# Three-piece score visits in batches 3 to 7, with a piece placed in two of TensorE's single PSUM banks

## The chip, the cores and the metric

One core of one Trainium2 chip. The metric is the time of one execution in device microseconds, the median of several runs. A ratio is the mean time of one kernel's fast runs over the mean of the fast runs of the kernel before from the same rounds, so it is not quite the ratio of the medians quoted beside it. A profile's span is some 1.7 us shorter than the time of its run. The profiled run of the kernel before took 342.69 us, 1.6 above its median. Microseconds are written us.

## The reference, cut to what matters

```python
B, H, S, Nb, D = 8, 8, 576, 16, 64
k_all = concat([beacon_k, k]); v_all = concat([beacon_v, v])     # 592 keys
scores = q @ k_all.T / sqrt(D), causal on the 576 ordinary keys  # ... per batch and head
a = exp(scores - max); a /= a.sum(-1)
x = (a @ v_all) as 4608 tokens x 512
h = relu(x @ w_in); out = (h * h) @ w_out                        # d_ff = 2048
```

Attention of eight batches feeds an MLP on all tokens. The MLP needs far more TensorE time than the attention, and the kernel lays the attention of one batch between MLP chunks of earlier ones.

## The kernel before

Every piece of work is an `Op`, and a list scheduler inside the Python program (`Order.run`) decides while the kernel is built in which order the operations of each engine stand. It plays with estimated durations, and it hands out PSUM banks from pools. PSUM is TensorE's output memory. The kernel divides it into eight banks: two "strips" of two banks for scores, and four single banks `ps` for everything else (MLP, values, transposes).

```python
strips = [psum.tile([128, 2, 512], FP32, name=f"strip{i}") for i in range(2)]
ps = [psum.tile([128, 512], FP32, name=f"ps{i}") for i in range(4)]
...
order = Order(pools={"strip": range(2), "ps": range(4), "stg": range(NSTG)}, limits={"av": 2, "tp": 2})
```

The scores of a batch (four pairs of heads) are cut into 13 pieces of 512 columns. For each piece TensorE makes 64-row matmuls for two heads side by side (one head in each bank of a strip), and ScalarE takes exp of both banks in one instruction of 1024 columns. A *visit* is a run of score matmuls on TensorE between other work; here it has up to two pieces, so a batch has seven visits.

```python
def emit_scores(b, mms, st):
    for pr, c, t0, t1, at in mms:
        for hj in range(2):
            nc.tensor.matmul(st[:, hj, at:at + t1 - t0], kT[b % 2][64*hj:64*hj+64, pr, ...],
                             qT[b % 2][64*hj:64*hj+64, pr, t0:t1], start=True, stop=True)

def add_exp(name, qk, s, at, width, prio):
    def emit(e):
        nc.scalar.activation(pt[:, :, at:at + width], strips[qk.slots[s]][:, :, 0:width], AF.Exp, ...)
    ...
            if len(parts) == 2 or n == NPC - 1 and b not in CROSS:
                opened.clear()                 # the visit is full
```

A single bank is filled by TensorE and then emptied ("evicted") by ScalarE or VectorE: ReLU of an MLP group, the reciprocal and the product that normalize the values, or a copy.

The softmax here doesn't subtract the row's maximum and nothing guards it: scores larger than these inputs give would overflow.

## Time and profile before

| | before |
|---|---|
| time, median | 341.06 us (340.79 to 341.26) |
| TensorE (PE) busy | 335.6 of 341.0 us, 98% |
| ScalarE (ACT), VectorE (DVE) busy | 56%, 51% |
| chain that ended last | 97% PE |
| score runs on PE in the built order | 65 |

The page of the kernel before: the busy line of section 1 (engine, busy us, share of the span, instructions) and the chain that ended last (section 4).

```profile
PE 335.6 (98%) x3197; PEld 187.4 (55%) x3197; DVE 173.0 (51%) x389; ACT 190.3 (56%) x270; POOL 92.5 (27%) x145
...
PE 97%; DVE 1%; issue 0%; ACT 0%; DVEq 0%
```

The view of waits of the same kernel, TensorE alone (who waited for whom: us in total, times, longest us). These three lines are all.

```profile
PE ps L286 <- DVE warm L293: 1.1, 1, 1.1
PE ps L878 <- DVE g L896: 0.7, 1, 0.7
PE ps L475 <- ACT g L894: 0.5, 1, 0.5
```

TensorE is the bound, and nearly all of its time is its own. A change helps if TensorE streams less or loses less between instructions, and a new wait of TensorE should be paid in full.

The chain of the kernel before in order of time shows what a visit looks like (start us, length us, what); L611 are scores, L715 values, L878 and L916 the MLP:

```profile
138.20 1.83 PE ps L916 x8
140.04 0.46 PE ps L715 x15
140.50 0.86 PE ps L916 x4
141.36 0.55 PE strip L611 x10
141.91 0.57 PE ps L715 x15
```

Four MLP matmuls of 512 columns take 0.86 us, fifteen value matmuls 0.46, but 0.57 after the visit at 141.36. Start times of single matmuls in the trace show the visit's fixed cost better: the last matmul before a visit lasts 0.096 us longer than its columns need, the visit's last pair 0.10 longer, and the first matmul after it 0.01 longer. That is 0.205 us for a visit of any size.

### The profile page before, as it was taken

The page shows a single profiled execution, that of the slowest core. Times are in us where ns is not written, and L with a number is a line of the kernel's source. Part 1 is how long each engine was busy: PE and PEld are TensorE (multiplying, and loading weights), DVE is VectorE, ACT ScalarE, POOL GpSimd, SP SyncE. Part 2 cuts the span into 40 slices and gives each one's busy share as a digit, 9 for nine tenths or more (in the row PEclk, how much of TensorE's full clock was granted, in tenths as well). Part 3 has the DMA queues.
Part 4 walks back from the last instruction along what each step waited for, and adds up shares of the span by engine and source line. Part 5 has one row for each costly group of instructions (what it writes and reads, how often), then busy time and mean ns, then how long its engine had stood idle before and what let it go on. Part 6 is the DMA issues. An engine that isn't in the chain of part 4 may idle for free.

```text
span 341.0 us, 7787 instructions
## 1 busy us (share of the span) xinstructions
PE 335.6 (98%) x3197; PEld 187.4 (55%) x3197; DVE 173.0 (51%) x389; ACT 190.3 (56%) x270; POOL 92.5 (27%) x145
## 2 busy tenths in 40 slices
PE   8999999999999999999999999999999999999996
PEld 7677665544564555555467855545454544444444
DVE  3886886238465982477336743767255502401400
ACT  2886765367647765576456653675367316514721
POOL 9773712406504533042315041504000000000000
PEclk9999999999999999999999999999999999999999
DMA  8999987999999999799989998997310131011003
GB/s 143 209 185 213 209 149 165 224 241 217 170 204 238 219 172 189 162 238 188 201 154 220 226 215 131 217 233 125 105 62 2 29 104 62 0 60 65 0 2 123
DMA packets 143953, 51.72 MB, mean 152 GB/s; under 512 B 130702, under 2 KB 138798, under 8 KB 143918
## 3 DMA queue, kind: packets, MB, share of 16 engines
q1 hardware_dynamic: 135375, 42.19, 61.8%
q0 software_dynamic: 7904, 8.69, 15.0%
q8 instruction: 25, 0.41, 0.5%
q10 hardware_dynamic: 639, 0.36, 0.4%
q14 instruction: 10, 0.08, 0.1%
HBM read 37.22 MB, written 9.44 MB: 137 GB/s over the span
## 4 chain that ended last, share of the span: by engine, by line
PE 97%; DVE 1%; issue 0%; ACT 0%; DVEq 0%
PE ps L878 36%; PE ps L916 36%; PE ps L715 9%; PE strip L611 9%; PE ps L286 3%; PE ps L475 2%; PE ps L782 1%; PE ps L828 1%; DVE g L903 1%; PE ps L472 0%; ACT g L894 0%; PE ps L420 0%; DVE g L896 0%; ACT osb L316 0%; DVE g L292 0%
## 5 line engine op out<-in xcount | busy, mean ns | idle before, releaser
L878 PE MATMUL ps<-xT,w_in 128*128 128x512 bf16 (+3 forms) x704 | 134.0, 340 | 0.7 <-DVE g L896 0.7
L916 PE MATMUL ps<-w_out,g 128*128 128x512 bf16 x560 | 131.4, 379 | 0.0
L620 ACT ACTIVATE pt<-strip 128x1024 bf16<-128x1024 f32 (+3 forms) x107 | 101.9, 1000 | 43.2 <-PE strip L611 42.8
L878 PEld LDWEIGHTS <-w_in 128*128 128x128 bf16 x704 | 65.5, 98 | 52.9 <-issue 2.0
L894 ACT ACTIVATE g<-ps 128x512 bf16<-128x512 f32 (+2 forms) x120 | 67.5, 563 | 45.2 <-PE ps L878 44.7
L903 DVE TENSOR_TENSOR g<-g 128x1024 bf16<-128x1024 bf16 (+2 forms) x80 | 54.2, 684 | 68.6 <-ACT g L894 67.7
L916 PEld LDWEIGHTS <-g 128*128 128x128 bf16 x560 | 51.0, 98 | 54.8 <-issue 1.7
L318 POOL CAST qk_area<-stg 128x512 bf16<-128x512 f32 (+2 forms) x60 | 40.1, 676 | 66.1 <-DMA stg<-in_q_dram 33.7
L318 POOL CAST vb<-stg 128x512 bf16<-128x512 f32 (+1 forms) x40 | 26.4, 671 | 67.8 <-DMA stg<-in_v_dram 49.3
L316 ACT COPY osb<-ps 128x512 f32<-128x512 f32 (+2 forms) x28 | 15.8, 567 | 50.8 <-PE ps L916 48.6
L715 PEld LDWEIGHTS <-pt 128*128 128x128 bf16 (+1 forms) x960 | 35.7, 98 | 11.0 <-issue 2.1
L715 PE MATMUL ps<-vb,pt 128*128 128x65 bf16 (+1 forms) x960 | 39.8, 194 | 0.0
L689 DVE TENSOR_TENSOR pt<-pt,tri 128x512 bf16<-128x512 bf16 x64 | 31.6, 503 | 10.2 <-ACT pt L620 9.0
L611 PE MATMUL strip<-qT,kT 64*128 64x208 bf16 (+15 forms) x596 | 34.2, 239 | 0.0
L734 DVE TENSOR_TENSOR xn<-ps,rcp 128x320 bf16<-128x320 f32 (+2 forms) x64 | 31.5, 492 | 2.3
L611 PEld LDWEIGHTS <-kT 64*128 64x128 bf16 x596 | 19.0, 94 | 21.2 <-issue 19.9
L732 DVE RECIPROCAL rcp<-ps 128x5 f32<-128x5 f32 (+2 forms) x64 | 12.2, 190 | 34.5 <-PE ps L715 34.2
L896 DVE TENSOR_SCALAR g<-ps 128x512 bf16<-128x512 f32 (+2 forms) x40 | 23.4, 601 | 8.6 <-PE ps L878 7.4
L318 DVE COPY osb<-ps 128x512 f32<-128x512 f32 (+1 forms) x10 | 6.5, 651 | 31.0 <-PE ps L916 19.0
L286 PE MATMUL ps<-g 128*128 128x256 bf16 (+1 forms) x83 | 12.0, 302 | 1.1 <-DVE warm L293 1.1
L362 POOL DMA_DIRECT2D stg<-in_v_dram x10 | 8.6, 866 | 6.4 <-DMA w_in<-in_moe_w_in_dram 5.3
L286 PEld LDWEIGHTS <-g 128*128 128x128 bf16 x83 | 7.9, 122 | 3.5 <-issue 1.5
(40 smaller groups left out, 82.2 us busy)
## 6 DMA issues: line engine op xcount, KB each, us to landing
out_dram<-osb SPq DMA_DIRECT2D x17, 512.0 KB, 4.3
stg<-in_q_dram SPq DMA_DIRECT2D x24, 256.0 KB, 5.0
stg<-in_k_dram SPq DMA_DIRECT2D x18, 256.0 KB, 5.3
stg<-in_v_dram SPq DMA_DIRECT2D x18, 256.0 KB, 4.7
w_in<-in_moe_w_in_dram POOLq DMA_DIRECT2D x4, 512.0 KB, 8.7
w_out<-in_moe_w_out_dram POOLq DMA_DIRECT2D x4, 512.0 KB, 11.2
stg<-in_v_dram POOLq DMA_DIRECT2D x6, 256.0 KB, 8.3
stg<-in_k_dram SPq DMA_DIRECT2D x6, 224.0 KB, 4.1
```

Of the source, the lines that this page charges most:

```text
L286: nc.tensor.matmul(ps[bank][:, 0:cols], g[1][:, 0, 0:128], g[1][:, 0, 0:cols], start=True, stop=True)
L318: eng[e].tensor_copy(dst, src)
L611: nc.tensor.matmul(st[:, hj, at:at + t1 - t0], kT[b % 2][hp, pr, 128 * c:128 * c + 128], qT[b % 2][hp, pr, t0:t1], start=True, stop=True,)
L620: nc.scalar.activation(pt[:, :, at:at + width], strips[qk.slots[s]][:, :, 0:width], AF.Exp, bias=0.0, scale=scale)
L689: nc.vector.tensor_tensor(out=d, in0=d, in1=tri[:, m0:m0 + m, :][:, None].to_broadcast([128, 2, m, 128]), op=ALU.min)
L715: nc.tensor.matmul(a[:, at + (t - tl[0]) * (D + 1):at + (t - tl[0] + 1) * (D + 1)], P[0:rr, hj, o:o + 128], vb[b % 2][0:rr, c, 2 * pr + hj ...
L734: nc.vector.tensor_tensor(out=xn[b % 2].rearrange("p t (h d) -> p h t d", d=D)[:, h0:h0 + nh, tl[0]:tl[0] + nt], in0=a[:, :, :, 0:D], in1= ...
L878: nc.tensor.matmul(h[:, lo - spans[0][0]:hi - spans[0][0]], w_in_sb[:, mc, ft * 128:(ft + 1) * 128], xT[:, mc, lo % RING:lo % RING + hi - lo],
L894: nc.scalar.activation(dst, h, AF.Relu, bias=0.0, scale=1.0)
L896: nc.vector.tensor_scalar(out=dst, in0=h, scalar1=0.0, scalar2=None, op0=ALU.max)
L903: nc.vector.tensor_tensor(out=d, in0=d, in1=d, op=ALU.mult)
L916: nc.tensor.matmul(o, G[:, fc, ts * 128:(ts + 1) * 128], w_out_sb[:, fc, :], start=(fc == 0), stop=(fc == NFT - 1))
```

## The change

Intent: fewer visits. In batches 3 to 7 the 13 pieces go in visits of 2, 3, 3, 3 and 2 pieces. The two strips hold two pieces, and the third goes into single banks 0 and 1 while a visit needs them. An exp reads two banks in one instruction, so the two banks are made halves of one tile. The core of the diff, with comments added here:

```diff
     strips = [psum.tile([128, 2, 512], FP32, name=f"strip{i}") for i in range(2)]
-    ps = [psum.tile([128, 512], FP32, name=f"ps{i}") for i in range(4)]
+    strips.append(psum.tile([128, 2, 512], FP32, name="strip2"))
+    ps = [strips[2][:, 0, :], strips[2][:, 1, :]] + [psum.tile([128, 512], FP32, name=f"ps{i}") for i in (2, 3)]
...
+    PAIR = [0, 1]
...
+                    if e == "PE" and any(o.wide and len(self.pools["strip"]) == 2 and o.gate(self) for o in avail[e]):
+                        held = self.PAIR          # a three-piece visit is due: keep both banks for it
...
+                            if op.wide and not all(x in self.pools["ps"] for x in self.PAIR):
+                                continue
...
+    PLAN = ((2,2,2,2,2,2,1),(2,2,2,2,2,2,1),(2,3,3,3,2),(2,3,3,3,2),(2,3,3,3,2),(2,3,3,3,2),(2,3,3,3,2))
+    FREE = 1
...
+            runs = [(0,), (1, 2)] if size == 3 else [tuple(range(size))]
+                # visits from batch 2 on in a fixed order; the second run right behind the first
```

The matmuls, the exps and all other arithmetic are the same in number and size.

More of the change, by code (lines that the diff above doesn't have):

```diff
@@ L21 @@
                  "take", "give", "gate", "held", "slots", "dma", "pe_time", "behind", "followers",
-                 "sync", "insts", "late")
+                 "sync", "insts", "late", "wide")
     def __init__(self, name, engs, dur, emit, prio=0.0, deps=(), take=None, give=None,
@@ L27, in __init__ @@
         self.late = late
+        self.wide = False
         self.engs = engs if isinstance(engs, (tuple, list)) else (engs,)
@@ L106, in run @@
                     pool, cls = from_op.take[:2]
+                    if from_op.slots[which] == 2 and pool == "strip":
+                        self.pools["ps"] += self.PAIR
+                        continue
                     self.pools[pool].append(from_op.slots[which])
@@ L117, in run @@
                     fallback = None
+                    held = ()
+                    if e == "PE" and any(o.wide and len(self.pools["strip"]) == 2 and o.gate(self) for o in avail[e]):
+                        held = self.PAIR
                     for op in avail[e]:
@@ L122, in run @@
                             pool, cls, need = op.take
-                            if len(self.pools[pool]) < need:
+                            if len([x for x in self.pools[pool] if pool != "ps" or x not in held]) < need:
+                                continue
+                            if op.wide and not all(x in self.pools["ps"] for x in self.PAIR):
                                 continue
@@ L154, in run @@
                         pool, cls, need = op.take
-                        op.slots = [self.pools[pool].pop(0) for _ in range(need)]
+                        op.slots = [x for x in self.pools[pool] if pool != "ps" or x not in held][:need]
+                        self.pools[pool] = [x for x in self.pools[pool] if x not in op.slots]
+                        if op.wide:
+                            op.slots.insert(0, 2)
+                            self.pools["ps"] = [x for x in self.pools["ps"] if x not in self.PAIR]
                         op.held = (pool, cls, op.slots[0])
@@ L616, in emit_scores, with add_exp @@
                 )
-    def add_exp(name, qk, s, at, width, prio):
+    def add_exp(name, qk, s, at, width, prio, done):
         def emit(e):
@@ L621, in emit @@
                                  AF.Exp, bias=0.0, scale=scale)
-        return add(name, "ACT", 0.18 + 2 * width / 1200.0, emit, prio=prio, deps=[qk], give=(qk, s))
+        return add(name, "ACT", 0.18 + 2 * width / 1200.0, emit, prio=prio, deps=[done], give=(qk, s))
     exps_of = {}
-    CROSS = ()
     SHIFT = 0.25
-    opened = []
-    def new_visit(b, n):
-        pos = HP * b + 512.0 * n / PW
-        parts = []
-        def emit(e):
-            for s, (bb, m) in enumerate(parts):
-                emit_scores(bb, PIECES[m], strips[qk.slots[s]])
-        qk = add(f"qk{b}.{n}", "PE", 0.2, emit, prio=100.0 * pos - 1000.0, take=("strip", "strip"), gate=gate_at(pos - SHIFT))
-        opened.append((qk, parts))
+    PLAN = ((2,2,2,2,2,2,1),(2,2,2,2,2,2,1),(2,3,3,3,2),(2,3,3,3,2),(2,3,3,3,2),(2,3,3,3,2),(2,3,3,3,2))
+    last_qk = []
+    FREE = 1
     def add_batch(b):
@@ L644, in add_batch @@
             qk_ops[p], av_ops[p], exps_of[p] = [], [], []
-        for n in range(NPC):
-            if not opened:
-                new_visit(b, n)
-            qk, parts = opened[0]
-            parts.append((b, n))
-            qk.take = ("strip", "strip", len(parts))
-            qk.dur += sum(t1 - t0 for _, _, t0, t1, _ in PIECES[n]) / 2400.0
-            pairs = sorted({mm[0] for mm in PIECES[n]})
-            e = add_exp(f"exp{b}.{n}", qk, len(parts) - 1, 512 * n, 512,
-                        1.0e-2 * (HP * b + 512.0 * n / PW) - 30.0)
-            for pr in pairs:
-                p = HP * b + pr
-                for o in deps_of(b, pr, 0) + av_ops[p - HP]:
-                    if o not in qk.need:
-                        qk.need.append(o)
-                qk_ops[p].append(qk)
-                exps_of[p].append(e)
-            if len(parts) == 2 or n == NPC - 1 and b not in CROSS:
-                opened.clear()
+        n = 0
@@ new lines, in add_batch, with emit @@
+        for size in (PLAN[b - 1] if isinstance(PLAN[0], tuple) else PLAN):
+            pos = HP * b + 512.0 * n / PW
+            box = {}
+            runs = [(0,), (1, 2)] if size == 3 else [tuple(range(size))]
+            for k, run in enumerate(runs):
+                def emit(e, run=run, n=n, box=box):
+                    for s in run:
+                        emit_scores(b, PIECES[n + s], strips[box["qk"].slots[s]])
+                qk = add(f"qk{b}.{n + run[0]}", "PE", 0.2 / len(runs) + 512 * len(run) / 2400.0, emit,
+                         prio=-1.0e6 if k else 100.0 * pos - 1000.0, behind=[qk] if k else last_qk[-1:] if size == 3 or b > FREE else [],
+                         take=None if k else ("strip", "strip", min(size, 2)), gate=None if k else gate_at(pos - SHIFT))
+                last_qk.append(qk)
+                if k == 0:
+                    qk.wide = size == 3
+                    box["qk"] = qk
+                for s in run:
+                    e = add_exp(f"exp{b}.{n + s}", box["qk"], s, 512 * (n + s), 512, 1.0e-2 * (pos + 0.1 * s) - 30.0, qk)
+                    for pr in sorted({mm[0] for mm in PIECES[n + s]}):
+                        p = HP * b + pr
+                        for o in deps_of(b, pr, 0) + av_ops[p - HP]:
+                            if o not in box["qk"].need:
+                                box["qk"].need.append(o)
+                        qk_ops[p].append(qk)
+                        exps_of[p].append(e)
+            n += size
@@ L664, in add_batch @@
+        assert n == NPC
         for pr in range(HP):
@@ L679, in add_pair @@
                 qk_ops[p].append(qk)
-                exps.append(add_exp(f"exp{p}.{n}.{i}", qk, 0, PW * p + off, width, (base + i) * 1.0e-4 - 400.0))
+                exps.append(add_exp(f"exp{p}.{n}.{i}", qk, 0, PW * p + off, width, (base + i) * 1.0e-4 - 400.0, qk))
             add_phase(b, pr, p, n, ph, base, exps)
```

## The prediction

> **What bounds the kernel.** TensorE. On the page PE is busy 335.6 of 341.0 us (98%) at full granted clock, and the chain of waits is 97% PE. The waits view shows PE stopped by another engine only three times (1.1, 0.7, 0.5 us), all in the first 45 us. VectorE (51%) and ScalarE (56%) have room on average.
>
> **What the change removes.** A score visit puts 64-row matmuls between 128-row ones. From start times in the trace: four 512-column matmuls before a visit take about 0.960 us instead of 0.864; the last matmul pair of a visit lasts about 0.10 us longer than its columns, the first matmul after it 0.01. A visit thus costs 0.205 us whatever its size (one piece 0.33 us, two 0.55). This agrees with the Trainium skill, "TensorEngine Tiling (Array Packing)", Tiling Modes, Key Properties: changing the tiling mode drains TensorE; the page gives no time. In the built order the score runs on TensorE go from 65 to 55, with 3197 matmuls in both. The two parts of a three-piece visit stand next to each other. Saving: 10 x 0.205 = 2.05 us, all on the chain.
>
> **What it adds.** ScalarE, VectorE and DMA do the same work. But single banks 0 and 1 become halves of one tile. In the waits of the built program, dependencies are now kept for this tile, not per bank: TensorE writing one half waits for the eviction of the other (about 60 places), and evictions of one half wait for a later TensorE write of the other (about 50). This holds in every batch, and the kernel's own scheduler, which treats the banks as separate, doesn't know it.
>
> Cost of one: from the end of streaming to a ReLU's start the trace shows 0.20 us, the ReLU takes 0.597 (exp 1.024, norm 0.19+0.49), from its end to the freed matmul 0.055. So a TensorE write needs 0.85 us of other TensorE work behind the write being evicted; 1.45 where two ReLUs stand in line. After the start-up the kernel before always has over 1.2 us. The new order has some seven places with 0.45 to 0.5 us (0.36 to 0.46 stall each, one of them 1.0 with two ReLUs), some fifteen with 0.86 to 1.3 us behind norms or pairs of evictions (0.1 to 0.3 each), and one with 0.89 us behind an exp (0.4). Estimate: 3.6 + 2.2 + 0.4 = 6 us, all on the chain; I take 5.8, since some may overlap.
>
> Holding two of four banks for a wide visit also thins the buffering; outside the cases above I expect little.
>
> **Prediction.** 341.0 - 2.05 + 5.8 = 344.8 us. Range 342.0 to 348.0. Chances: faster by over 2%: 0.01; within 2%: 0.86; slower by over 2%: 0.13.
>
> **What would show it right.** 55 score runs; the 0.205 us per visit unchanged. Idle PE time before L892, L930 and L729 (MLP and value matmuls) in many waits of 0.1 to 1.0 us for ScalarE L908/L331 and VectorE L748/L910, on the merged tile, the sum 4 to 8 us; some in batches 1 and 2, where visits are as before. PE busy near 333 us.
>
> **What would make it wrong.** If those waits are mostly met in time, it is 339 to 340 us. If ScalarE, with three exps (3.1 us) in line, delays ReLUs more than counted, or stalls follow one another, it is 348 or more. If the visits' switch cost is not saved, add 2.

## The result, and the profile after

| | before | after |
|---|---|---|
| time, median | 341.06 us (340.79 to 341.26) | 350.11 us (349.66 to 350.80) |
| ratio, 95% interval | | 1.0268 [1.0246, 1.029] |
| profiled span | 341.0 us | 348.8 us |
| chain that ended last, PE share | 97% | 86% |

The change is slower by 2.7%, outside the range predicted. The page of the changed kernel, the same two lines:

```profile
PE 334.5 (96%) x3156; PEld 190.4 (55%) x3197; DVE 168.5 (48%) x385; ACT 188.3 (54%) x274; POOL 91.3 (26%) x145
...
PE 86%; DVE 7%; ACT 4%; issue 2%; DVEq 0%; ACTq 0%
```

PE busy fell a little while the time rose, and VectorE and ScalarE have entered the chain with 11% of the span. The fall of PE busy by 1.1 us means nothing: 41 of the 3197 matmul records are missing from this trace, and some 40 gaps of 0.05 us, 2 us in all, stand where they were. (The weight loads, PEld, are complete.) The view of waits, TensorE alone, its first seven lines; line numbers are shifted: L892 and L930 are the MLP, L729 the values, L908 the ReLU on ScalarE, L331 its copies, L748 the normalization on VectorE:

```profile
PE strip L892 <- ACT g L908: 1.5, 4, 0.7
PE strip L301 <- DVE warm L308: 1.1, 1, 1.1
PE strip L892 <- ACT xT L331: 0.9, 1, 0.9
PE strip L729 <- ACT xT L331: 0.7, 1, 0.7
PE ps L729 <- DVE pt L703: 0.6, 1, 0.6
PE strip L301 <- DVE qT L333: 0.6, 1, 0.6
PE strip L729 <- DVE xn L748: 0.3, 2, 0.2
```

Nearly all are writes of `strip`, the name under which the merged tile shows. The seven lines add up to 5.7 us and the whole view to 7.1, against 2.3 in the kernel before: some 4.8 us are new. That lies within the 4 to 8 us that the prediction named as a sign of being right, and yet the loss is larger. The view lists no gap under 0.15 us, and the profile counts a matmul of 512 columns as busy for 0.379 us while such matmuls follow one another every 0.216, so the first 0.16 us of each stall is hidden in "busy". The Trainium skill, "Trainium Kernel Development and Optimization", Performance Expectations, warns that matmul busy time is a bad metric for how close a kernel is to the limit of the hardware, because matmuls are pipelined. `e2_visits_only` below has the same matmuls in the same order, also with 41 records missing, and PE is busy 329.8 us in it; the changed kernel counts 4.7 us more for the same work. Where two kernels have the same TensorE order, the difference of start times of the n-th weight load is the better measure, and it is used below.

### The profile page after: what moved, and what is told of

The parts are those of the page before. It is cut to its first block, busy times and chain, and to the rows that moved or that the text cites. A ratio compares the mean times of both kernels' runs of the same rounds, so it can differ in the third digit from the quotient of the medians.

```text
span 348.8 us, 7757 instructions
## 1 busy us (share of the span) xinstructions
PE 334.5 (96%) x3156; PEld 190.4 (55%) x3197; DVE 168.5 (48%) x385; ACT 188.3 (54%) x274; POOL 91.3 (26%) x145
## 4 chain that ended last, share of the span: by engine, by line
PE 86%; DVE 7%; ACT 4%; issue 2%; DVEq 0%; ACTq 0%
PE ps L930 22%; PE strip L892 17%; PE ps L892 16%; PE strip L930 12%; PE strip L626 7%; PE strip L729 4%; PE ps L729 3%; ACT g L908 2%; DVE g L910 2%; DVE pt L703 2%; PE ps L301 2%; DVE xn L748 2%; PE strip L301 1%; ACT xT L331 1%; ACT pt L635 1%
## 5 line engine op out<-in xcount | busy, mean ns | idle before, releaser
L892 PEld LDWEIGHTS <-w_in 128*128 128x128 bf16 x704 | 65.8, 98 | 55.0 <-issue 4.5
L917 DVE TENSOR_TENSOR g<-g 128x1024 bf16<-128x1024 bf16 (+2 forms) x80 | 52.5, 664 | 72.7 <-ACT g L908 72.2
L930 PE MATMUL ps<-w_out,g 128*128 128x512 bf16 x350 | 85.3, 379 | 1.1 <-issue 0.2
L930 PEld LDWEIGHTS <-g 128*128 128x128 bf16 x560 | 52.4, 98 | 60.0 <-issue 3.1
L892 PE MATMUL ps<-xT,w_in 128*128 128x512 bf16 (+3 forms) x347 | 72.6, 341 | 0.7
L892 PE MATMUL strip<-xT,w_in 128*128 128x512 bf16 (+3 forms) x340 | 68.7, 338 | 3.6 <-ACT g L908 1.5
L908 ACT ACTIVATE g<-strip 128x512 bf16<-128x512 f32 (+2 forms) x59 | 30.7, 555 | 41.4 <-PE strip L892 28.3
L930 PE MATMUL strip<-w_out,g 128*128 128x512 bf16 x186 | 46.0, 379 | 1.2 <-ACT xT L331 0.3
L908 ACT ACTIVATE g<-ps 128x512 bf16<-128x512 f32 (+2 forms) x62 | 35.3, 571 | 16.2 <-PE ps L892 13.8
L729 PEld LDWEIGHTS <-pt 128*128 128x128 bf16 (+1 forms) x960 | 36.3, 97 | 13.5 <-issue 3.6
L331 ACT COPY osb<-strip 128x512 f32<-128x512 f32 (+1 forms) x13 | 7.1, 570 | 32.1 <-PE strip L930 16.0
L331 ACT COPY osb<-ps 128x512 f32<-128x512 f32 (+1 forms) x17 | 9.6, 567 | 26.2 <-PE ps L930 14.1
L729 PE MATMUL strip<-vb,pt 128*128 128x65 bf16 (+1 forms) x492 | 20.6, 194 | 1.2 <-ACT xT L331 0.7
L729 PE MATMUL ps<-vb,pt 128*128 128x65 bf16 (+1 forms) x468 | 19.4, 194 | 0.6 <-DVE pt L703 0.6
L748 DVE TENSOR_TENSOR xn<-strip,rcp 128x320 bf16<-128x320 f32 (+2 forms) x34 | 16.6, 488 | 1.2
```

Of the source, the lines that this page charges most:

```text
L331: nc.scalar.copy(dst, src)
L729: nc.tensor.matmul(a[:, at + (t - tl[0]) * (D + 1):at + (t - tl[0] + 1) * (D + 1)], P[0:rr, hj, o:o + 128], vb[b % 2][0:rr, c, 2 * pr + hj ...
L748: nc.vector.tensor_tensor(out=xn[b % 2].rearrange("p t (h d) -> p h t d", d=D)[:, h0:h0 + nh, tl[0]:tl[0] + nt], in0=a[:, :, :, 0:D], in1= ...
L892: nc.tensor.matmul(h[:, lo - spans[0][0]:hi - spans[0][0]], w_in_sb[:, mc, ft * 128:(ft + 1) * 128], xT[:, mc, lo % RING:lo % RING + hi - lo],
L908: nc.scalar.activation(dst, h, AF.Relu, bias=0.0, scale=1.0)
L917: nc.vector.tensor_tensor(out=d, in0=d, in1=d, op=ALU.mult)
```

## The experiments

Theory A: the loss is made of waits that follow from banks 0 and 1 being one tile, in every batch. Theory B: the loss is made by the wide visits themselves, which hold two of four single banks and put three exps in line on ScalarE.

### The tile alone, and the visits alone

`e1_tile_only` is the kernel before with the merged tile and nothing else:

```diff
-    ps = [psum.tile([128, 512], FP32, name=f"ps{i}") for i in range(4)]
+    pair = psum.tile([128, 2, 512], FP32, name="pair")
+    ps = [pair[:, 0, :], pair[:, 1, :]] + [psum.tile([128, 512], FP32, name=f"ps{i}") for i in (2, 3)]
```

Its orders on TensorE, VectorE and ScalarE are those of before, instruction for instruction, so no visit is changed.

> The kernel before with one edit: single banks 0 and 1 are halves of one tile; visits and the order of every engine's instructions are those of before (compared instruction by instruction). Theory A (the loss comes from dependencies kept per tile): 348 to 353 us, with new TensorE stalls of 0.1 to 1.0 us whose sum is 7 to 12 us, at the start-up too. Theory B (the loss comes from the wide visits themselves: two of four banks held, three exps in a row on ScalarE): 341 us, no new stalls.

Measured: 352.93 us (352.68 to 353.71), ratio 1.0343 [1.0315, 1.0372], as theory A had it. The view of waits, TensorE alone, its first four lines (2.3 us in the whole view before, 9.2 now; L917 and L879 are the MLP):

```profile
PE pair L917 <- DVE g L897: 1.2, 2, 0.8
PE pair L287 <- DVE warm L294: 1.1, 1, 1.1
PE pair L917 <- DVE xn L735: 1.1, 3, 0.4
PE pair L879 <- ACT g L895: 0.9, 3, 0.4
```

`e2_visits_only` is the changed kernel with four separate tiles. The wide piece lies in two of them, and its exp is two instructions:

```diff
+            if qk.slots[s] == 2:
+                for hj in range(2):
+                    nc.scalar.activation(pt[:, hj, at:at + width], ps[hj][:, 0:width], AF.Exp, bias=0.0, scale=scale)
+                return
```

TensorE's and VectorE's orders are those of the changed kernel.

> The changed kernel with four separate single-bank tiles; the wide piece lies in two of them and its exp is two instructions of 512 columns, one for each bank. TensorE's and VectorE's orders are those of the changed kernel. Theory A: 338.5 to 340.5 us (before minus 2.05, plus at most about 1 for 15 exps that take some 0.17 us more). Theory B: 347 us or more, as the changed kernel.

Measured: 338.40 us (338.02 to 339.37), ratio 0.9923 [0.9897, 0.9949]. That is 0.1 us below the range of theory A and far from theory B. The gain of 0.8% is clear of noise.

This settles A against B. The tile costs 11.9 us where no visit was touched, and without it the wide visits gain 2.7 us. The split exp costs nothing that shows: the 30 halves take 0.597 us each and ScalarE is busy 57% of that run.

### Twice the dose

`e4_two_pairs` also merges banks 2 and 3 (`ps = [pairs[i // 2][:, i % 2, :] for i in range(4)]`), again with the order of before.

> As e1, but banks 2 and 3 are one tile too: the dose of shared-tile dependencies doubled, order of instructions again that of before. Theory A: the loss of e1 about doubled or more, 355 to 368 us. Theory B: 341 us.

Measured: 365.91 us (365.26 to 368.35), ratio 1.0733 [1.0695, 1.0771]. That is 24.9 us over before, against 11.9 for one pair: the loss goes with the number of merged tiles.

### What a visit costs

`e3_single_visits` gives the kernel before one-piece visits in batches 3 to 7, 93 score runs instead of 65:

```diff
-            if len(parts) == 2 or n == NPC - 1 and b not in CROSS:
+            if len(parts) == (1 if b >= 3 else 2) or n == NPC - 1 and b not in CROSS:
```

> The kernel before with one-piece visits in batches 3 to 7: 93 score runs on TensorE instead of 65. If a visit costs 0.205 us of TensorE time whatever its size, 28 x 0.205 = 5.7 us more: 346 to 348 us, no new stalls. If the switch were hidden elsewhere, 341 to 343 us.

Measured: 347.23 us (345.98 to 349.00), ratio 1.0176 [1.0140, 1.0213]. TensorE's waits add up to 2.3 us in its view, as before, so no new stalls are in it. The difference of 6.2 us over 28 visits is 0.22 us a visit; the interval of the ratio allows 0.17 to 0.26.

`e8_twos_control` is `e2_visits_only` with `PLAN = ((2,2,2,2,2,2,1),) * 7`: all that is left of the change is the fixed order of visits and small shifts in priorities.

> e2_visits_only with visits of two pieces in every batch: 65 score runs, no wide piece, all banks separate tiles; what is left of the change is the fixed order of visits from batch 2 on and small shifts in priorities. If the gain of e2_visits_only is the ten visits alone, 340.5 to 341.1 us, that is 2.0 to 2.7 us above it. If part of it came from the other order, 339 to 340 us.

Measured: 340.30 us (340.06 to 342.74), ratio 0.9980 [0.9947, 1.0014]. The time lies between the two guesses and meets neither. Against 0.9923 of `e2_visits_only`, the ten visits are worth 0.0057 of 341 us, 1.9 us; the two intervals just touch, so the value is rough (0.5 to 3.4 us if the two intervals are combined). What is left of the 2.7 us isn't told from noise.

`e5_wide_everywhere` is `e2_visits_only` with `PLAN = ((2,3,3,3,2),) * 7`, so 51 score runs.

> As e2_visits_only (separate tiles, wide piece's exp in two), with the visits 2, 3, 3, 3, 2 in batches 1 and 2 too: 51 score runs instead of 55. If each visit costs 0.205 to 0.22 us, 0.8 to 0.9 us less than e2_visits_only: about 337.5 us, the best so far. If holding two banks costs more in the early batches, where loads and transposes crowd the engines, 338.5 us or more.

Measured: 345.22 us (343.82 to 347.04), ratio 1.0113 [1.0077, 1.0149]. It was run on another chip. The guess of 337.5 us missed: by the ratios it is 6.5 us slower than `e2_visits_only`. TensorE's waits in this run (L800 are TensorE's transposes of attention output, L752 the normalization, L711 and L707 masks) are of another sort:

```profile
PE ps L800 <- DVE xn L752: 3.6, 4, 1.1
PE ps L300 <- DVE warm L307: 1.1, 1, 1.1
PE ps L934 <- issue: 0.6, 4, 0.2
PE ps L733 <- DVE pt L711: 0.6, 2, 0.4
PE ps L733 <- DVE pt L707: 0.4, 1, 0.4
```

The waits for L752, L711 and L707 stand at 62 to 69 us and at 107 us. There the chain of this run goes through masks, values, normalization and transposes on VectorE and TensorE in turn, with no MLP work between. Why the order left none there was not tested. What the run shows is that wide visits in batches 1 and 2 lose more than fewer visits save.

### Is it the order that doesn't know?

`e6_order_knows` keeps the merged tile and the wide visits, and lets the scheduler know of it:

```diff
+    def other_half_busy(self, op, slot, now):     # asked before an op may start
+        if slot not in (0, 1):
+            return False
+        return (self.writes if "PE" not in op.engs else self.reads)[1 - slot] > now + 1e-9
```

> The changed kernel with its one tile, but its scheduler now knows it: it starts no TensorE write of one half while an issued eviction of the other half is in flight, and no eviction of one half while an issued TensorE write of the other is. If the loss comes from waits that the order was made in ignorance of, most of it goes: 341 to 346 us. If the tile costs time by itself (for instance by its place in memory), about 350 us as the changed kernel.

Measured: 343.72 us (343.10 to 344.20), ratio 1.0065 [1.0035, 1.0095]. It was run on another chip. By the ratios, an order made with knowledge of the tile gets back 6.9 of the 11.8 us that lie between the changed kernel and `e2_visits_only`. Of the rest it is only known that waits remain, among them 65 of the third kind below, of which the scheduler was not told; halves that are forbidden for a while also leave fewer banks. No run separates the two.

### Which waits

In the built changed kernel, I listed what each instruction on one half of the merged tile waits for and counted the waits that name an instruction on the other half. There are three kinds: 76 TensorE writes wait for an eviction of the other half, 73 evictions wait for a TensorE write of the other half (15 of them exps, which need both halves anyway), and 45 evictions on ScalarE or VectorE wait for an eviction of the other half by the other engine. The prediction had costed the first two, counting about 60 and 50 of them, and overlooked the third.

The third kind in the changed kernel, in its timeline (start us, length us, engine, line, operation, operands, idle before it and what ended it):

```profile
24.20 0.31 PE L796 MATMUL strip<-ident,xn 128*128 128x128 bf16 x3
24.35 0.57 PE L892 MATMUL ps<-xT,w_in 128*128 128x240 bf16 x4
24.61 0.20 DVE L746 RECIPROCAL rcp<-strip 128x6 f32<-128x6 f32 x1 [0.45 <-ACT pt L635]
24.84 0.56 DVE L748 TENSOR_TENSOR xn<-strip,rcp 128x384 bf16<-128x384 f32 x1
25.48 0.44 ACT L331 COPY xT<-strip 128x336 bf16<-128x336 bf16 x1 [1.29 <-DVE xn L748]
25.97 0.26 PE L892 MATMUL strip<-xT,w_in 128*128 128x240 bf16 x1 [0.86 <-ACT xT L331]
```

The same instructions in the kernel before:

```profile
23.70 0.31 PE L782 MATMUL ps<-ident,xn 128*128 128x128 bf16 x3
23.86 0.57 PE L878 MATMUL ps<-xT,w_in 128*128 128x240 bf16 x4
23.90 0.20 DVE L732 RECIPROCAL rcp<-ps 128x6 f32<-128x6 f32 x1
24.05 0.44 ACT L316 COPY xT<-ps 128x336 bf16<-128x336 bf16 x1 [0.34 <-PE ps L782]
24.13 0.56 DVE L734 TENSOR_TENSOR xn<-ps,rcp 128x384 bf16<-128x384 f32 x1
24.55 0.58 PE L878 MATMUL ps<-xT,w_in 128*128 128x240 bf16 x4
```

Before, the copy on ScalarE waits only for TensorE, and runs beside VectorE's normalization of another bank. After, ScalarE sits idle for 1.29 us until VectorE has read the other half, and TensorE, which needs the copied bank, is idle 0.86 us. (Not all of this is the third kind: with only the first two kinds put back, in `d_counted_kinds` below, TensorE lost 0.35 us at this place.)

The first two kinds, where two ReLUs stand in line, in the changed kernel:

```profile
197.68 1.91 PE L892 MATMUL strip<-xT,w_in 128*128 128x256 bf16 x16
199.42 0.62 PE L729 MATMUL ps<-vb,pt 128*128 128x65 bf16 x15
199.62 1.09 ACT L908 ACTIVATE g<-strip 128x512 bf16<-128x512 f32 x2 [1.85 <-PE strip L892]
200.76 1.03 PE L892 MATMUL strip<-xT,w_in 128*128 128x256 bf16 x8 [0.72 <-ACT g L908]
201.63 0.63 PE L729 MATMUL ps<-vb,pt 128*128 128x65 bf16 x15
201.83 0.60 ACT L908 ACTIVATE g<-strip 128x512 bf16<-128x512 f32 x1 [1.12 <-PE strip L892]
202.48 1.03 PE L892 MATMUL strip<-xT,w_in 128*128 128x256 bf16 x8 [0.22 <-ACT g L908]
```

and the same stretch in `e2_visits_only`, with the same TensorE order (L896 for L892, L733 for L729, L912 for L908):

```profile
189.48 1.91 PE L896 MATMUL ps<-xT,w_in 128*128 128x256 bf16 x16
190.55 0.60 ACT L912 ACTIVATE g<-ps 128x512 bf16<-128x512 f32 x1 [0.74 <-PE ps L896]
191.22 0.62 PE L733 MATMUL ps<-vb,pt 128*128 128x65 bf16 x15
191.43 0.60 ACT L912 ACTIVATE g<-ps 128x512 bf16<-128x512 f32 x1 [0.28 <-DVE rcp L750]
191.68 1.04 PE L896 MATMUL ps<-xT,w_in 128*128 128x256 bf16 x8
192.56 0.63 PE L733 MATMUL ps<-vb,pt 128*128 128x65 bf16 x15
192.75 0.60 ACT L912 ACTIVATE g<-ps 128x512 bf16<-128x512 f32 x1 [0.73 <-PE ps L896]
193.02 1.04 PE L896 MATMUL ps<-xT,w_in 128*128 128x256 bf16 x8
```

The sixteen MLP matmuls fill two banks, eight matmuls each. In the changed kernel the first ReLU waits until both halves are written, so two ReLUs run one behind the other, 1.09 us in all, and TensorE stands idle for 0.72 us of it. In the other kernel each ReLU runs as soon as its own bank is full, the first at 190.55, beside TensorE. (The view puts the second ReLU's release down to VectorE; in the built program it waits for TensorE alone.)

To weigh the kinds, four kernels put them back by hand; the comment in the diff is added. Each is `e2_visits_only`, with its separate banks and its exact order, plus explicit waits between banks 0 and 1:

```diff
+    def other_half(self, e, half, mine):          # after each op on bank 0 or 1 is emitted
+        for (what, ee, h), first in self.last.items():
+            kind = ("write" if e == "PE" else "read", what)
+            if h != half and ee != e and kind in self.KINDS:
+                self.wait_for(mine[0], first)
+        self.last["write" if e == "PE" else "read", e, half] = mine[-1]
```

`KINDS` is ("write", "read") for the first kind, ("read", "write") for the second, ("read", "read") for the third. The built programs have 68, 56 and 44 such waits, nearly the counts of the merged tile.

> e2_visits_only with its four separate banks and its exact order of instructions, and with waits added by hand between banks 0 and 1 as the one tile has them, of all three kinds: TensorE's write of one bank waits for issued evictions of the other, an eviction for an issued TensorE write of the other, and an eviction on one engine for an issued eviction of the other bank on the other engine. If waits are the whole cost of the tile: 348.5 to 351 us, as the changed kernel (350.1). If the tile costs by something else too, clearly under 348.

> Only the two kinds of waits that the prediction costed (write after eviction, eviction after write). If the prediction's 5.8 us for them was right and the rest comes from the third kind, which it did not count: 343.5 to 345.5 us. If the two kinds were themselves mis-sized and the third is idle: 348 to 350.5 us.

> Only the third kind: an eviction on ScalarE waits for an issued eviction of the other bank on VectorE, and the reverse (44 places). ScalarE and VectorE have room, so by itself 338.5 to 340.5 us; if it is what the prediction missed, and adds without the others, 343 us or more.

> Only TensorE's writes wait for issued evictions of the other bank (68 places). If this kind alone makes most of the cost of the two counted ones: 341.5 to 344 us. If evictions waiting for later writes matter as much, 339 to 341 us.

| kernel | waits put back | time, median | ratio to before, 95% interval | over `e2_visits_only` |
|---|---|---|---|---|
| `e2_visits_only` | none | 338.40 us | 0.9923 [0.9897, 0.9949] | |
| `d_evict_evict` | third kind | 339.46 us | 0.9953 [0.9932, 0.9973] | 1.1 us |
| `d_write_after_evict` | first | 342.80 us | 1.0050 [1.0025, 1.0075] | 4.4 us |
| `d_counted_kinds` | first and second | 346.71 us | 1.0162 [1.0139, 1.0186] | 8.3 us |
| `d_all_waits` | all three | 350.85 us | 1.0278 [1.0249, 1.0308] | 12.4 us |
| the changed kernel | (merged tile) | 350.11 us | 1.0268 [1.0246, 1.0290] | 11.7 us |

The waits are the whole cost of the tile: with all three put back the time is that of the changed kernel within the intervals, though the banks are separate tiles and the exps are split. So neither the tile's place nor the shape of the exp carries a loss of its own that these runs could see. The kinds aggravate each other. The second adds 3.9 us to the first (it was not run alone). The third is worth 1.1 us by itself and 4.1 us on top of the other two; a likely reason, not tested, is that a late eviction matters only where TensorE waits for it. Both guesses for `d_counted_kinds` (343.5 to 345.5, and 348 to 350.5) missed: it lies between, so the two counted kinds were sized too small *and* the third was missing.

Where the time goes, as the lag of the n-th weight load of TensorE behind that of `e2_visits_only` (same order; spans of the profiled runs):

| by this time of `e2_visits_only` | changed kernel | `d_counted_kinds` | `d_evict_evict` |
|---|---|---|---|
| 45 us | 3.6 us | 1.8 us | 0.8 us |
| 120 us | 6.5 us | 3.3 us | 1.3 us |
| 195 us | 9.5 us | 5.9 us | 1.5 us |
| 270 us, and to the end | 11.4 us | 7.6 us | 1.5 us |

A third of the loss has come by 45 us, half of it (5.8 us) before the first wide visit at 106 us, and none after 270 us, where attention is over.

## Why the prediction was wrong, point by point

- **TensorE is the bound, each new wait is paid in full.** Right: the chain was 97% PE before, and waits put back by hand came out as time.
- **A visit costs 0.205 us, ten fewer save 2.05 us.** Right: 0.22 us a visit by the single visits (6.2 us over 28), about 1.9 us for the ten by the control. The Trainium skill, "TensorEngine Tiling (Array Packing)", Tiling Modes, Key Properties, says that changing the mode drains TensorE; the runs agree that a switch costs time, and say how much, but no trace shows a drain as such.
- **The merged tile ties the banks together in every batch, and the scheduler doesn't know.** Right: the tile alone costs 11.9 us in the order of before, and an order that is told gets 6.9 us back.
- **Holding two banks in a wide visit costs little.** Right in batches 3 to 7: `e2_visits_only` holds them too and gains 2.7 us. In batches 1 and 2 wide visits cost 6.5 us, which the change avoids and the prediction didn't touch.
- **"Estimate: 3.6 + 2.2 + 0.4 = 6 us ... I take 5.8."** This is the step that failed: what the waits on the merged tile cost. The term is 11.7 us (the changed kernel over `e2_visits_only`). Two parts of the gap are known:
  - A kind of wait was left out, eviction for eviction across ScalarE and VectorE. On top of the others it costs 4.1 us. The place at 24 to 26 us shown above is one; the same copy at 55 us, again behind a normalization on the other half, lost 0.83 us, and 0.11 with only the counted kinds put back. The Trainium skill would have pointed to it: "PSUM — Partial Sum Buffer", PSUM bank collisions raise a hardware error, says that the compiler back end's scheduler adds dependencies between any two instructions on different engines that touch one bank and quadrant, reads and writes alike, ScalarE against VectorE too. It says this of one bank; here the wait is kept between two banks of one tile.
  - The two counted kinds cost 8.3 us rather than 5.8. The cost of one place was not too small: at five of its places behind ReLUs, all after 150 us, the weight loads of the changed kernel fall back by 0.88 us (two ReLUs in line, 1.0 expected) and by 0.38, 0.20, 0.19 and 0.19 us (0.36 to 0.46 expected). What was missing were places: the built program has 76 and 73 waits, not about 60 and 50, and the estimate speaks of the time "after the start-up", while in the first 45 us the counted kinds alone lost 1.8 us. From 45 us on they lost 5.8 us (7.6 less 1.8 in the table above), which is the whole estimate; as the places just named lost less than expected, other places must have lost more, so this agreement is partly luck. Which places those are stays open.
- **What would make it wrong: "stalls follow one another, it is 348 or more".** The time did come out there, and one kind does make another worse, but the prediction named no third kind, and three exps in line by themselves cost nothing to be seen in `e2_visits_only`.

## What to carry to other kernels

Making two PSUM banks one tile can tie together instructions that have nothing to do with each other: look at the waits in the built program, for all three pairs (write after read, read after write, read after read across engines), before trusting a scheduler or an estimate that knows banks only. Here two exps of 512 columns instead of one of 1024 let the banks stay separate tiles, and turned a loss of 2.7% into a gain of 0.8%. Count such waits from the first instruction on, and don't add their costs up one by one: the third kind cost 1.1 us alone and 4.1 us beside the others.

## What the Trainium skill lacked or had wrong

- "TensorEngine Tiling (Array Packing)", Tiling Modes, gives no time for the drain at a mode switch. Here the cost was 0.205 us for a visit of 64-row matmuls between 128-row ones (0.096 before it, 0.10 at its end, 0.01 after), 0.22 us by the run with 28 more visits.
- "TensorE: Matmul & The Clock Gate", Back-to-back issue gap, gives about 131 ns per matmul as the sustained rate for 512 columns with a weight load for each, and says that N/2.4 + 2.5 over-counts there. In all thirteen traces here such streams run at 216 ns from start to start (median), which is what the formula gives, and what the same page has earlier in its picture of the phases.
- "PSUM — Partial Sum Buffer", PSUM bank collisions, says to guard by bank and quadrant. No page says that a tile of two banks may be guarded as a whole: here 76, 73 and 45 waits between its banks, 11.7 us. With separate tiles the kernel ran without them, correct, in 338.4 us.
